# A sliding-window attention and MLP-mixer kernel: u turned by DMA in five of eight batches, and the hand-written order rewritten

## Chip, cores, metric

The kernel runs on one core of one Trainium2 chip. The metric is the device time of one execution in microseconds (us). Twelve executions of the kernel before gave a median of 300.88 us (298.99 to 302.43).

## What is computed

The reference, cut to what matters:

```
q, k, v: [8 batches, 8 heads, 576 tokens, 64]        float32
scores = q @ k.T / 8 + alibi bias, kept where 0 <= i - j < 128
attn   = softmax(scores);  x = (attn @ v) as [8, 576, 512]
h  = relu(x.T @ w_tok1) @ w_tok2        w_tok1 576x256, w_tok2 256x576
u  = x + h.T
h2 = relu(u @ w_ch1) @ w_ch2            w_ch1 512x1536, w_ch2 1536x512
out = u + h2
```

Only a band of 128 tokens takes part in each row of scores, so the two channel products (the last line but one) are most of the arithmetic.

## The kernel before

576 tokens are four chunks of 128 and a tail of 64. The work of each batch is cut into named steps, and five strings (PROLOGUE, FIRST, SECOND, PERIOD, LAST; lines 23 to 47) say by hand in which order the steps are issued. PERIOD is run for batches 2 to 6. A name without a tick is a step of the current batch b; each tick adds one batch, so `S20''` in batch b is a score step of batch b + 2. There is no scheduler: every engine runs its instructions in the order in which the strings issue them, and a step that waits holds up what stands behind it on the same engine. `emit` (line 809) walks the strings.

The steps, with the engine and the line of their main instruction:

- `q l` (193), `v` and `L` (183, 186), `LW`, `G`, `H` (665, 693, 732): loads from HBM with a cast to bf16, issued on POOL. `q`, `l` load a pair or two pairs of heads of q and k for batches 0 and 1; `Lq`, `Lk` load q and k of a later batch by tokens into `qn`, `kn` (four loads of 128 tokens and a tail each); `v0` to `v4` load v; `LW` loads w_tok1 and w_tok2; `G0` to `G2` load thirds of w_ch1 (512 KB each in SBUF), `H0`, `H1` halves of w_ch2 (768 KB each). The first two head pairs of batch 0 come in float32 on SP's queue (723) and are cast by DVE and ACT (`cq`, `ck`, 728).
- `M`, `m`: masks of the alibi bias, from `dist` that `J` makes on POOL. `I` makes the identity.
- `A`, `AT` (227, 252): TensorE turns q and k of batches 0 and 1 by head pair. `Zq`, `Zk` (211, 214): for batches 2 to 7 DMA transposes on SP's queue turn `qn`, `kn` into `qT`, `kT`.
- `S`kb j (280 to 293): scores of key chunk kb for four heads (j) on TensorE, exp on ACT out of a PSUM pair `psS`, product with the mask on DVE (299) one step later.
- `p` (572), `P` (339, 343, 371): attention times v. The first is by head pair, for batch 0, the others by query chunk. DVE takes reciprocals of the sums (587, 352) and scales.
- `k`, `K` (610, 404): first token product. `u`, `U`, `UT` (628, 429, 440): second token product, with x added on DVE (431), which gives `ub`, that is u.
- `x`, `X` (645, 461): u is turned, 128 x 128 blocks at a time, into `utb`, as `C` needs it with channels on the partitions. TensorE does it: four transposes for a chunk of 128 tokens, then one copy out of PSUM by ACT or DVE (464). A batch has four such chunks, X0 to X3.
- `C` (471) and `T` (486): channel product 1, twelve steps of four matmuls of 512 columns; the relu goes to DVE for the numbers in DVE_RELU (474), else to ACT (477).
- `D` (519) and `E` (541): channel product 2, three parts a chunk, four matmuls of 512 columns a part; DVE adds u (524) and SP's queue stores (525).
- `W`n (656): n matmuls on zeros that nobody reads.

PSUM has two pairs `psS` and three single tiles `psM` in rotation. SP's queue carries the float32 loads, the DMA transposes and the output stores, in the order of the strings. POOL carries all other loads. `utrans` (448) holds both ways of turning u: for batches in U_DMA it issues one DMA transpose for two chunks (451), at X0 and X2, and nothing at X1 and X3. In the kernel before, U_DMA is empty.

Of the kernel before, what the change touches and what calls it, by code (L numbers as in the profile page):

```python
# [10 lines left out]
ACT = mybir.ActivationFunctionType  # L11
# [4 lines left out]
PE_BATCHES = 2  # L16
CH2_PARTS = 3
MASK_LATER = 1
U_DMA = ()
U_ACT = (0,)  # L20
X_DVE = (3,)
K_DVE = (1,)
PROLOGUE = """
l1 O q0 I J q23 M0 l0 l23 FC qt G0 M1 m0 ck1 v0 cq0 M2 v1 LC q1 ck0 M3 cq1 v2 A0 v3 A1 S00 v4
S20 A2 AT S10 A3 m1 S30 LW q01' G1 q23' S21 S01 S11 W1 p0 l01' l23' p1 k0 v1' S31 k1 v3' qt' G2
v1'' u0 u1 Lk'' v4' v2' p2 x1 v0' p3 H1 H0 Lq'' k2 x0 u2 k3 v3'' ek A0' v4''' u3
"""
FIRST = """
UT x2 A2' v4'' x3 e1 A3' C4 C6 v0'' Zk'' Zq'' AT' S21' S11' A1' Lq''' T1 C1 C8 ex S00' S01' C9
C2 S20' C7 P0' T0 S10' C3 S30' S31' e2 C5 v2'' C0 v2''' Lk''' P1' C11 v0''' C10 P3' D00 P2' D01  # L30
P4' v3''' v1''' D02 E2 K0' K1' D10 D11 U1' D12 U3' X1' U2' UT' D20 D21 E1 U0' D30 S11'' S00''
D31 S10'' D22 S01'' T1' D32 E0 S20'' X3' X0' P0'' Zq'''
"""
SECOND = """
X2 T0 v4''' Zk'' P1' C5 S30' C3 C11 C0 Lk''' S31' S21' C9 C2 C7 C10 C6 P3' C1 v0''' C8 v2''' C4
v3''' D00 D01 P2' P4' D02 Lq''' K0' v1''' S01'' S20'' K1' D10 D11 D12 U3' U2' UT' U1' U0' X2'
S11'' S10'' X1' D20 X0' D21 D22 S21'' S00'' D30 E0 E1 X3' E2 D31 D32 P0''
# [7 lines left out]
C0 C6 C7 C1 C3 C2 C8 C5 C11 C4 C9 C10 D00 D20 D21 D10 T0 D01 D02 D22 D11 D12 T1 E0 E1 E2 D30 D31  # L45
D32
"""
VROW = 96
NPB = 9
SPLIT = (0, 2, 3, 5, 7)  # L50
x_DVE = (1, 2, 3)
k_DVE = (0, 1)
AK_DVE = (0, 3, 4, 5, 6, 7)
AQ_ACT = (0, 4, 6)
DVE_RELU = (2, 3, 6, 8, 10, 11)


@with_exitstack
def kernel(
# [102 lines left out]
    def later(n, fn):  # L162
        pend.append([n, fn])
# [94 lines left out]

    qrot = [0]
    probs = {}  # L260
    tok1_banks = {}

    def score(b, kb, j):

        i = b % 2

        def f():
            n = qrot[0]  # L270
# [286 lines left out]
    def pv_hp(hp):  # L557
        def f():
            E = 2 * (D + 1)
            vt = vp[0]  # L560
            psO = S2()
            for bank in range(2):
                first = True
                for qb in (2 * bank, 2 * bank + 1):
                    for i in range(2):
                        oi = psO[:, bank, (qb % 2) * E + i * (D + 1):(qb % 2) * E + (i + 1) * (D + 1)]
                        if qb > 0:
                            nc.tensor.matmul(
                                oi, lhsT=prob(0, qb - 1, 2 * hp + i, 1),
                                rhs=vt[:, qb - 1, 2 * hp + i, 0:D + 1], start=first, stop=False)  # L570
# [165 lines left out]
    def names(b):  # L736
# [40 lines left out]
        if b == 0:  # L777
# [74 lines left out]
```

The softmax here doesn't subtract the row's maximum and nothing guards it: scores larger than these inputs give would overflow.

## Time and profile before

| | |
|---|---|
| median of 12 executions | 300.88 us |
| the profiled execution | 299.84 us |
| its span on the core | 298.1 us |
| TensorE (PE) busy | 282.9 us, 95% |
| VectorE (DVE) busy | 172.7 us, 58% |
| ScalarE (ACT) busy | 129.0 us, 43% |
| POOL busy, with its load instructions | 99.6 us, 33% |
| mean granted TensorE clock | 0.989 |

The profile page is read as follows. A row of 40 digits cuts the span into equal slices (7.45 us here) and gives the busy share in tenths; PEclk is the granted TensorE clock in tenths of full speed. Group lines name the line, the engine, the operation, out<-in, the shape and the count, then busy time and mean duration, then idle time of the engine just before them and what ended it. The mean duration of a matmul is its latency; consecutive matmuls overlap, so what one costs a busy TensorE is the distance of starts. The chain of waits follows the run back from its last instruction; its pieces, given as start and length, don't overlap, so they show this distance.

### The profile page before, as it was taken

The page shows a single profiled execution, that of the slowest core. Times are in us where ns is not written, and L with a number is a line of the kernel's source. Part 1 is how long each engine was busy: PE and PEld are TensorE (multiplying, and loading weights), DVE is VectorE, ACT ScalarE, POOL GpSimd, SP SyncE. Part 2 cuts the span into 40 slices and gives each one's busy share as a digit, 9 for nine tenths or more (in the row PEclk, how much of TensorE's full clock was granted, in tenths as well). Part 3 has the DMA queues.
Part 4 walks back from the last instruction along what each step waited for, and adds up shares of the span by engine and source line. Part 5 has one row for each costly group of instructions (what it writes and reads, how often), then busy time and mean ns, then how long its engine had stood idle before and what let it go on. Part 6 is the DMA issues. An engine that isn't in the chain of part 4 may idle for free.

```text
span 298.1 us, 6583 instructions
## 1 busy us (share of the span) xinstructions
PE 282.9 (95%) x2757; PEld 159.5 (54%) x2757; DVE 172.7 (58%) x341; ACT 129.0 (43%) x203; POOL 99.6 (33%) x128
## 2 busy tenths in 40 slices
PE   1989997999999999999999999999999999999995
PEld 0568654546455456555564556555554556554453
DVE  2788776547756546485647636485647536543221
ACT  6853784038415534245615444345515444022210
POOL 8776871159209808800690008600000000000000
PEclk9969999999999999999999999999999999999999
DMA  7999999999999999952999169913501120110023
GB/s 175 178 194 185 172 180 159 147 167 180 129 145 141 174 206 157 142 94 77 177 155 134 42 150 158 142 52 114 118 2 70 49 61 0 36 72 35 2 90 86
DMA packets 138076, 35.38 MB, mean 119 GB/s; under 512 B 125248, under 2 KB 133568, under 8 KB 138048
## 3 DMA queue, kind: packets, MB, share of 16 engines
q0 software_dynamic: 103152, 17.41, 77.0%
q1 hardware_dynamic: 34896, 17.57, 25.3%
q8 instruction: 21, 0.34, 0.5%
q14 instruction: 7, 0.06, 0.1%
HBM read 35.85 MB, written 9.44 MB: 152 GB/s over the span
## 4 chain that ended last, share of the span: by engine, by line
PE 82%; DMA 12%; ACT 2%; POOL 1%; issue 1%; DVE 1%; SPq 0%
PE psM L519 27%; PE psM L471 25%; DMA WC<-in_moe_w_ch_dram 11%; PE psM L429 4%; PE psM L404 4%; PE psS L280 4%; PE psM L541 3%; PE psT L486 3%; PE psM L461 2%; PE psS L343 2%; DMA kf<-in_k_dram 2%; PE psS L339 2%; ACT pe L293 1%; PE psS L371 1%; PE psM L500 1%; PE psM L413 1%
## 5 line engine op out<-in xcount | busy, mean ns | idle before, releaser
L471 PE MATMUL psM<-utb,WC 128*128 128x512 bf16 x384 | 90.2, 379 | 0.2 <-ACT r L477 0.2
L519 PE MATMUL psM<-WC,r 128*128 128x512 bf16 x372 | 88.2, 379 | 1.8 <-DMA WC<-in_moe_w_ch_dram 1.8
L293 ACT ACTIVATE pe<-psS 128x1024 bf16<-128x1024 f32 (+1 forms) x69 | 62.7, 964 | 37.4 <-PE psS L280 30.0
L519 PEld LDWEIGHTS <-r 128*128 128x128 bf16 x372 | 34.3, 98 | 40.2 <-issue 4.4
L471 PEld LDWEIGHTS <-WC 128*128 128x128 bf16 x384 | 34.7, 98 | 37.5 <-issue 1.6
L474 DVE TENSOR_SCALAR r<-psM 128x512 bf16<-128x512 f32 x48 | 33.2, 691 | 27.5 <-PE psM L471 27.4
L299 DVE TENSOR_TENSOR pb<-pe,masks 128x1024 bf16<-128x1024 bf16 (+1 forms) x51 | 33.3, 658 | 21.0 <-ACT pe L293 20.9
L183 POOL DMA_DIRECT2D kn<-in_k_dram x24 | 21.1, 903 | 64.2 <-DMA kT<-kn 63.2
L477 ACT ACTIVATE r<-psM 128x512 bf16<-128x512 f32 x48 | 27.8, 601 | 27.3 <-PE psM L471 27.2
L524 DVE TENSOR_TENSOR ob<-psM,ub 128x512 f32<-128x512 f32 x31 | 21.4, 691 | 27.0 <-PE psM L519 26.7
L183 POOL DMA_DIRECT2D vp<-in_v_dram x32 | 29.0, 945 | 3.9 <-DMA qn<-in_q_dram 2.3
L183 POOL DMA_DIRECT2D qn<-in_q_dram x24 | 21.2, 918 | 9.6 <-DMA qT<-qn 9.6
L431 DVE TENSOR_TENSOR ub<-psM,xb 128x512 bf16<-128x512 f32 x28 | 18.7, 683 | 3.8 <-PE psM L429 3.8
L464 ACT COPY utb<-psM 128x512 bf16<-128x512 bf16 x21 | 12.3, 597 | 19.8 <-PE psM L461 19.7
L489 ACT ACTIVATE r2t<-psT 128x384 bf16<-128x384 f32 x16 | 7.9, 492 | 28.7 <-PE psT L486 28.7
L353 DVE TENSOR_TENSOR xb<-psS,rt 128x512 bf16<-128x512 f32 x28 | 19.4, 691 | 1.0
L280 PE MATMUL psS<-qT,kT 64*128 64x256 bf16 x192 | 16.5, 280 | 1.3 <-ACT pe L293 0.6
L422 ACT ACTIVATE r<-psM 128x512 bf16<-128x512 f32 x7 | 4.2, 598 | 27.5 <-PE psM L413 27.5
L343 PE MATMUL psS<-vp,pb 128*128 128x65 bf16 x224 | 15.7, 193 | 0.0
L429 PE MATMUL psM<-r,W 128*128 128x512 bf16 x56 | 15.4, 381 | 0.0
L343 PEld LDWEIGHTS <-pb 128*128 128x128 bf16 x224 | 13.6, 97 | 3.4
L352 DVE RECIPROCAL rt<-psS 128x8 f32<-128x8 f32 x28 | 5.7, 204 | 15.1 <-PE psS L343 15.1
(119 smaller groups left out, 321.1 us busy)
## 6 DMA issues: line engine op xcount, KB each, us to landing
out_dram<-ob SPq DMA_DIRECT2D x31, 256.0 KB, 2.0
vp<-in_v_dram POOLq DMA_DIRECT2D x32, 128.0 KB, 5.7
kn<-in_k_dram POOLq DMA_DIRECT2D x24, 128.0 KB, 5.3
qn<-in_q_dram POOLq DMA_DIRECT2D x24, 128.0 KB, 4.8
WC<-in_moe_w_ch_dram POOLq DMA_DIRECT2D x3, 512.0 KB, 8.4
WC<-in_moe_w_ch_dram POOLq DMA_DIRECT2D x2, 768.0 KB, 12.0
out_dram<-ob SPq DMA_DIRECT2D x10, 128.0 KB, 2.3
qs<-in_q_dram POOLq DMA_DIRECT2D x3, 256.0 KB, 6.6
```

The costliest lines, as they stand in the source:

```text
L183: nc.gpsimd.dma_start(out=dst, in_=src[b, :, c * P:(c + 1) * P, :].rearrange("h s d -> s h d"))
L280: nc.tensor.matmul(s[:, h, a * 256:(a + 1) * 256], lhsT=kT[i][r, kb, hp, :], rhs=qT[i][r, kb:kb + 2, hp, :], start=True, stop=True)
L293: nc.scalar.activation(out=e[:, h, :], in_=s[:, h, :], func=ACT.Exp, scale=scale)
L299: nc.vector.tensor_tensor(out=p[:, :].rearrange("p (h x) -> p h x", h=2)[:, h], in0=e[:, h, :], in1=masks[:, j, h].rearrange("p h g a x -> ...
L343: nc.tensor.matmul(ov, lhsT=prob(b, qb, h, 0), rhs=vt[:, qb, h, 0:D + 1], start=first, stop=(hh == 3))
L353: nc.vector.tensor_tensor(out=xb[b % 2][:, qb, :].rearrange("p (b h d) -> p b h d", b=2, h=4), in0=ov[:, :, :, 0:D], in1=rv[:, :, :, None] ...
L429: nc.tensor.matmul(t[:, :], lhsT=W2[:, j, c * P:(c + 1) * P], rhs=r1[b % 2][:, j, :], start=(j == 0), stop=(j == 1))
L471: nc.tensor.matmul(t[:, :], lhsT=WC1[:, cb, ht * P:(ht + 1) * P], rhs=utb[b % 2][:, :, cb, :], start=(cb == 0), stop=(cb == NCB - 1))
L474: nc.vector.tensor_scalar(out=r2[b % 2][:, ht, :], in0=t[:, :], scalar1=0.0, scalar2=None, op0=ALU.max)
L477: nc.scalar.activation(out=r2[b % 2][:, ht, :], in_=t[:, :], func=ACT.Relu)
L519: nc.tensor.matmul(t[:, :], lhsT=r2[b % 2][:, ht, c * P:(c + 1) * P], rhs=WC2[:, ht, :], start=(ht == 0), stop=(ht == NHT - 1))
L524: nc.vector.tensor_tensor(out=o[:, :], in0=t[:, :], in1=ub[b % 2][:, c, :], op=ALU.add)
```

## The change

Settings and orders are changed, one step is added, and two functions are edited:

- U_DMA becomes (3, 4, 5, 6, 7): in these batches u is turned by two DMA transposes (X2 first, then X0) on SP's queue. Batches 0, 1 and 2 keep TensorE.
- In PERIOD `Zq''` and `Zk''` stand together, `Zq''` first, ahead of the loads `Lk'''` and `Lq'''`; FIRST has the order `Lk'' Lq''`, then `Zq'' Zk''`, then `Lk''' ...`. X stands earlier in PERIOD.
- In PROLOGUE and FIRST all loads of w_ch1 and w_ch2 and of batch 1 stand ahead of the q, k and v of batch 2; the tokens' weights (`LW`) stand ahead of the first w_ch1 third. Fifteen matmuls on zeros (`W`) are issued instead of one, nine of them before `A0`. `A0'` to `A3'`, `AT'`, `S00'`, `S01'`, `S10'` and `T0` stand before the first `C`, which is now `C8`.
- The first score step of batch 0 is cut in two, by head pair (`s0`, `t0`); four score steps of batch 0 use two `psM` tiles instead of a `psS` pair, and all are exponentiated by halves.
- `pv_hp` takes one reciprocal of 12 columns instead of two of 4 and 6.
- Sharing between DVE and ACT is redone; DVE_RELU has eight numbers instead of six.

```diff
-U_DMA = ()
+U_DMA = (3, 4, 5, 6, 7)
...
-X_DVE = (3,)
-K_DVE = (1,)
+X_DVE = (1, 3)
+K_DVE = (0,)
 PROLOGUE = """
-l1 O q0 I J q23 M0 l0 l23 FC qt G0 M1 m0 ck1 v0 cq0 M2 v1 LC q1 ck0 M3 cq1 v2 A0 v3 A1 S00 v4
-S20 A2 AT S10 A3 m1 S30 LW q01' G1 q23' S21 S01 S11 W1 p0 l01' l23' p1 k0 v1' S31 k1 v3' qt' G2
-v1'' u0 u1 Lk'' v4' v2' p2 x1 v0' p3 H1 H0 Lq'' k2 x0 u2 k3 v3'' ek A0' v4''' u3
+J M3 FC l23 M0 M1 W1 q0 q23 I l0 M2 cq0 W1 ck0 m0 l1 O q1 ck1 cq1 qt W3 v0 W4 A0 W3 v1 v2 s0 A1
+W2 S20 v3 t0 A2 AT v4 S10 LW A3 S30 m1 S01 l01' S11 q01' p0 G1 l23' p1 G0 W1 qt' e1 S31 k0 q23'
+S21 G2 H0 k1 v2' ek LC p2 A1' H1 A0' p3 u0 k2 u1 x0 v3' v4' k3 u2
 """
 FIRST = """
-UT x2 A2' v4'' x3 e1 A3' C4 C6 v0'' Zk'' Zq'' AT' S21' S11' A1' Lq''' T1 C1 C8 ex S00' S01' C9
...
+x1 v0' ex u3 A3' A2' AT' v1' Lk'' Lq'' UT x2 S00' S01' x3 Zq'' Zk'' T0 Lk''' S10' C8 v0'' v3''
+C9 Lq''' S20' v0''' S21' v4'' C3 e2 C5 S31' S11' C0 C2 S30' C4 v2'' v4''' C7 P0' C11 P2' T1 C1
+C10 C6 E0 D00 P1' D01 P3' D02 v1'' v2''' P4' K0' K1' D10 E2 U1' D11 D12 Zq''' U2' v1''' UT' X1'
+U0' D30 D20 S20'' S11'' D21 D31 D32 Zk''' E1 D22 S01'' U3' S00'' X2'
 """
...
 PERIOD = """
-P1' T0 Zk'' C1 C6 C9 C10 S30' S31' C0 Zq'' C4 C7 P3' C5 P2' C3 C8 v1''' T1 C11 v3''' Lk''' P4'
-C2 K0' Lq''' K1' v2''' D00 D01 D02 v4''' S01'' S00'' U0' U2' D10 v0''' D11 D12 U1' S21'' S11''
-U3' D20 X1' D21 P0'' D22 X0' UT' S20'' S10'' X2' X3' D30 D31 D32 E0 E1 E2
+C7 T0 C4 C3 C0 S31' S30' Zq'' C8 C2 Zk'' C11 C9 P1' C1 C10 P2' P3' Lk''' C6 C5 Lq''' P4' v0'''
+K0' K1' S01'' S00'' D00 v2''' v1''' D01 D02 T1 U2' U1' UT' U0' v3''' U3' D20 X2' X3' X1' D21
+P0'' D10 D11 v4''' S11'' S10'' X0' D12 D30 D22 D31 S20'' S21'' E0 E1 D32 E2
 """
...
-SPLIT = (0, 2, 3, 5, 7)
+SPLIT = (1, 2, 3, 4)
+S_M = (0, 5, 6, 7)
...
-DVE_RELU = (2, 3, 6, 8, 10, 11)
+DVE_RELU = (0, 2, 3, 4, 5, 7, 10, 11)
...
+    def score_half(kb, a):
+        def f():
+            if a == 0:
+                n = qrot[0]
+                qrot[0] += 1
+                half[kb] = (S2(), pe[n % len(pe)], pb[n % len(pb)])
+                probs[0, kb, 0] = half[kb][2]
+            s, e, p = half[kb]
+            cs = slice(a * 256, (a + 1) * 256)
+            for h in range(2):
+                r = slice(h * D, (h + 1) * D)
+                nc.tensor.matmul(s[:, h, cs], lhsT=kT[0][r, kb, a, :],
+                                 rhs=qT[0][r, kb:kb + 2, a, :], start=True, stop=True)
+            nc.scalar.activation(out=e[:, :, cs], in_=s[:, :, cs], func=ACT.Exp, scale=scale)
...
-            s = S2()
+            apart = b == 0 and j * 4 + kb in S_M
+            t2 = None if apart else S2()
+            s = [M(), M()] if apart else [t2[:, 0, :], t2[:, 1, :]]
...
-                for bank, n in ((0, 4), (1, 6)):
-                    nc.vector.reciprocal(
-                        out=r[:, bank * 4:bank * 4 + n, None],
-                        in_=psO[:, bank, 0:n * (D + 1)].rearrange("p (h e) -> p h e", h=n)[:, :, D:D + 1])
+                rv = r[:, :].rearrange("p (b h) -> p b h", b=2)
+                nc.vector.reciprocal(
+                    out=rv[:, :, :, None],
+                    in_=psO[:, :, 0:6 * (D + 1)].rearrange("p b (h e) -> p b h e", h=6)[:, :, :, D:D + 1])
```

More of the change, by code (lines that the diff above doesn't have):

```diff
@@ L27 @@
+W2 S20 v3 t0 A2 AT v4 S10 LW A3 S30 m1 S01 l01' S11 q01' p0 G1 l23' p1 G0 W1 qt' e1 S31 k0 q23'
+S21 G2 H0 k1 v2' ek LC p2 A1' H1 A0' p3 u0 k2 u1 x0 v3' v4' k3 u2
 """
 FIRST = """
-UT x2 A2' v4'' x3 e1 A3' C4 C6 v0'' Zk'' Zq'' AT' S21' S11' A1' Lq''' T1 C1 C8 ex S00' S01' C9
-C2 S20' C7 P0' T0 S10' C3 S30' S31' e2 C5 v2'' C0 v2''' Lk''' P1' C11 v0''' C10 P3' D00 P2' D01
-P4' v3''' v1''' D02 E2 K0' K1' D10 D11 U1' D12 U3' X1' U2' UT' D20 D21 E1 U0' D30 S11'' S00''
-D31 S10'' D22 S01'' T1' D32 E0 S20'' X3' X0' P0'' Zq'''
+x1 v0' ex u3 A3' A2' AT' v1' Lk'' Lq'' UT x2 S00' S01' x3 Zq'' Zk'' T0 Lk''' S10' C8 v0'' v3''
@@ L33 @@
+C9 Lq''' S20' v0''' S21' v4'' C3 e2 C5 S31' S11' C0 C2 S30' C4 v2'' v4''' C7 P0' C11 P2' T1 C1
+C10 C6 E0 D00 P1' D01 P3' D02 v1'' v2''' P4' K0' K1' D10 E2 U1' D11 D12 Zq''' U2' v1''' UT' X1'
+U0' D30 D20 S20'' S11'' D21 D31 D32 Zk''' E1 D22 S01'' U3' S00'' X2'
 """
 SECOND = """
-X2 T0 v4''' Zk'' P1' C5 S30' C3 C11 C0 Lk''' S31' S21' C9 C2 C7 C10 C6 P3' C1 v0''' C8 v2''' C4
-v3''' D00 D01 P2' P4' D02 Lq''' K0' v1''' S01'' S20'' K1' D10 D11 D12 U3' U2' UT' U1' U0' X2'
-S11'' S10'' X1' D20 X0' D21 D22 S21'' S00'' D30 E0 E1 X3' E2 D31 D32 P0''
+X3 X0 T1 S30' S10' C3 C1 T0 C2 P0' C8 Lk''' C7 v3'' C5 S31' S21' C11 Lq''' v2''' C4 C10 C0 P4'
@@ L38 @@
+v0''' v4''' C9 C6 D00 P1' v3''' P3' D01 P2' D02 v1''' K0' K1' S01'' S20'' D10 D11 D12 U2' UT'
+U0' U3' S00'' U1' X0' S11'' X2' D20 D21 E0 S21'' S10'' D22 E1 X1' E2 P0'' D30 X3' D31 D32
 """
 PERIOD = """
-P1' T0 Zk'' C1 C6 C9 C10 S30' S31' C0 Zq'' C4 C7 P3' C5 P2' C3 C8 v1''' T1 C11 v3''' Lk''' P4'
-C2 K0' Lq''' K1' v2''' D00 D01 D02 v4''' S01'' S00'' U0' U2' D10 v0''' D11 D12 U1' S21'' S11''
-U3' D20 X1' D21 P0'' D22 X0' UT' S20'' S10'' X2' X3' D30 D31 D32 E0 E1 E2
+C7 T0 C4 C3 C0 S31' S30' Zq'' C8 C2 Zk'' C11 C9 P1' C1 C10 P2' P3' Lk''' C6 C5 Lq''' P4' v0'''
@@ L43 @@
+K0' K1' S01'' S00'' D00 v2''' v1''' D01 D02 T1 U2' U1' UT' U0' v3''' U3' D20 X2' X3' X1' D21
+P0'' D10 D11 v4''' S11'' S10'' X0' D12 D30 D22 D31 S20'' S21'' E0 E1 D32 E2
 """
 LAST = """
-C0 C6 C7 C1 C3 C2 C8 C5 C11 C4 C9 C10 D00 D20 D21 D10 T0 D01 D02 D22 D11 D12 T1 E0 E1 E2 D30 D31
+C7 T1 C0 C1 C2 C9 C6 C8 C10 C11 C4 C3 T0 C5 D00 E0 D01 D10 D02 E1 D11 D20 D21 D22 E2 D12 D30 D31
 D32
@@ L49 @@
 NPB = 9
-SPLIT = (0, 2, 3, 5, 7)
+SPLIT = (1, 2, 3, 4)
+S_M = (0, 5, 6, 7)
 x_DVE = (1, 2, 3)
-k_DVE = (0, 1)
-AK_DVE = (0, 3, 4, 5, 6, 7)
-AQ_ACT = (0, 4, 6)
-DVE_RELU = (2, 3, 6, 8, 10, 11)
+k_DVE = (0, 1, 3)
+AK_DVE = (2,)
+AQ_ACT = (0, 1, 4, 5, 7)
+DVE_RELU = (0, 2, 3, 4, 5, 7, 10, 11)
 @with_exitstack
@@ L260, with g @@
     probs = {}
+    half = {}
+    def score_half(kb, a):
[12 more added lines that the diff above has]
+            nc.scalar.activation(out=e[:, :, cs], in_=s[:, :, cs], func=ACT.Exp, scale=scale)
+            def g():
+                nc.vector.tensor_tensor(
+                    out=p[:, :].rearrange("p (h x) -> p h x", h=2)[:, :, cs], in0=e[:, :, cs],
+                    in1=masks[:, 0, :, a].rearrange("p h g x -> p h (g x)"), op=ALU.mult)
+            later(MASK_LATER, g)
+        return f
     tok1_banks = {}
@@ L279, in f @@
                     for h, r in enumerate(halves):
-                        nc.tensor.matmul(s[:, h, a * 256:(a + 1) * 256], lhsT=kT[i][r, kb, hp, :],
+                        nc.tensor.matmul(s[h][:, a * 256:(a + 1) * 256], lhsT=kT[i][r, kb, hp, :],
                                          rhs=qT[i][r, kb:kb + 2, hp, :], start=True, stop=True)
@@ L283, in f @@
                 for h, r in enumerate(halves):
-                    nc.tensor.matmul(s[:, h, a * P:(a + 1) * P], lhsT=kT[i][r, kb, hp, :],
+                    nc.tensor.matmul(s[h][:, a * P:(a + 1) * P], lhsT=kT[i][r, kb, hp, :],
                                      rhs=qT[i][r, kb, hp, :], start=True, stop=True)
@@ L288, in f @@
                         c = 256 + t * P + a * ST
-                        nc.tensor.matmul(s[:, h, c:c + ST], lhsT=kT[i][r, kb + t, hp, :],
+                        nc.tensor.matmul(s[h][:, c:c + ST], lhsT=kT[i][r, kb + t, hp, :],
                                          rhs=qT[i][r, NC, hp, 0:ST], start=True, stop=True)
-            parts = (slice(0, 1), slice(1, 2)) if b == 0 and j * 4 + kb in SPLIT else (slice(0, 2),)
-            for h in parts:
-                nc.scalar.activation(out=e[:, h, :], in_=s[:, h, :], func=ACT.Exp, scale=scale)
+            split = apart or b == 0 and j * 4 + kb in SPLIT
+            parts = (slice(0, 1), slice(1, 2)) if split else (slice(0, 2),)
+            for n, h in enumerate(parts):
+                nc.scalar.activation(out=e[:, h, :], in_=s[n][:, None, :] if split else t2[:, :, :],
+                                     func=ACT.Exp, scale=scale)
             probs[b, kb, j] = p
@@ L592, in g @@
                     in0=psO[:, :, 0:2 * E].rearrange("p b (q i e) -> p b q i e", q=2, i=2)[:, :, :, :, 0:D],
-                    in1=r[:, 0:8].rearrange("p (b q i) -> p b q i", b=2, q=2)[:, :, :, :, None].broadcast_to([P, 2, 2, 2, D]),
+                    in1=rv[:, :, 0:4].rearrange("p b (q i) -> p b q i", q=2)[:, :, :, :, None].broadcast_to([P, 2, 2, 2, D]),
                     op=ALU.mult)
-                nc.vector.tensor_tensor(out=rtt[:, :], in0=r[:, 8:10], in1=hm[:, :], op=ALU.mult)
+                nc.vector.tensor_tensor(out=rtt[:, :], in0=r[:, 10:12], in1=hm[:, :], op=ALU.mult)
                 nc.vector.tensor_tensor(
@@ L796, in names @@
             d["O"] = lambda: ones_v(0)
+            for kb in range(NC - 1):
+                d[f"s{kb}"], d[f"t{kb}"] = score_half(kb, 0), score_half(kb, 1)
             for j in range(2):
```

## The prediction

> **What bounds the kernel now.** First the page: which engine is full, and where not.
>
> ```profile
> PE 282.9 (95%) x2757; PEld 159.5 (54%) x2757; DVE 172.7 (58%) x341; ACT 129.0 (43%) x203; POOL 99.6 (33%) x128
> ...
> PE   1989997999999999999999999999999999999995
> ...
> PEclk9969999999999999999999999999999999999999
> DMA  7999999999999999952999169913501120110023
> ```
>
> TensorE is full except in the first seven slices (52 us) and in the last. The clock dips in the third slice. The DMA engines are full for 17 slices and mostly free from slice 31. Next the busy time by stretch (columns: PE, PEld, DVE, ACT, POOL, clock, DMA share, GB/s), cut at the first product (16.86), the first C (31.95), the first D (51.07) and, further on, at starts of periods:
>
> ```profile
> 16.86:31.95 15.09, 13.97 (x229) 11.97 (x228) 12.25 (x36) 6.40 (x14) 11.00 (x15) 0.78 1.53 193
> 31.95:51.07 19.12, 17.11 (x207) 9.28 (x205) 14.35 (x27) 13.85 (x21) 10.28 (x13) 1.00 1.70 168
> 106.15:138.20 32.05, 32.05 (x318) 17.82 (x315) 20.65 (x39) 14.38 (x21) 12.57 (x15) 1.00 1.29 139
> 138.20:173.06 34.86, 34.86 (x334) 19.22 (x331) 20.33 (x38) 14.81 (x22) 12.56 (x15) 1.00 1.08 124
> ```
>
> A period holds 32.05 us of work on TensorE and no idle time; an odd batch has E as well and takes 34.86 us. So in PERIOD only what leaves TensorE counts. Then the chain of waits, in order of time (start, length):
>
> ```profile
> 25.00 8.83 DMA WC<-in_moe_w_ch_dram
> ...
> 36.67 14.36 DMA WC<-in_moe_w_ch_dram
> 51.07 1.02 PE psM L519 x4
> ...
> 166.62 0.55 PE psM L461 x8
> 167.17 2.59 PE psM L519 x12
> ```
>
> Up to 51 us the loads set the pace: the last third of w_ch1 lands at 33.83, the last half of w_ch2 at 51.03, and D starts with it (TensorE waits 1.81 us there, by the list of waits). After that all is TensorE. A transposing matmul of u costs 0.55/8 = 0.069 us in the chain, a matmul of 512 columns 2.59/12 = 0.216, though the groups give their latency:
>
> ```profile
> L461 PE MATMUL psM<-ident,ub 128*128 128x128 bf16 x112 | 9.9, 220 | 0.6 <-DVE ob L524 0.6
> L464 ACT COPY utb<-psM 128x512 bf16<-128x512 bf16 x21 | 12.3, 597 | 19.8 <-PE psM L461 19.7
> ```
>
> Last, the DMA transposes of q and k, issued on SP's queue (start, length of the issue), and their landings:
>
> ```profile
> 38.15 8.01 SPq L211 DMA_TRANSPOSE kT<-kn  x1
> ...
> 71.06 5.06 SPq L211 DMA_TRANSPOSE qT<-qn  x1
> ...
> 174.58 1.45 SPq L211 DMA_TRANSPOSE kT<-kn  x1
> ```
> ```profile
> DMA to landing us min/median/max: 3.6/5.2/15.7
> ```
>
> One of these turns 16 blocks of 128 x 128. The 3.6 to 6.3 us are those from 106 us on; the 15.7 and 12.4 us are those issued at 38.15 and 71.06, with loads in full flight.
>
> **What the Trainium skill says.** "TensorE: Matmul & The Clock Gate", What's actually happening: the array runs at half clock until about 3.4 us of sustained work, and falls back after an idle window. The trace agrees: eight 128-column transposes took 0.64 us at 4.92 and 0.41 us at 28.29, and the third slice was granted 0.6. "VectorE: DVE Perf Modes", The three transpose paths: 1309 ns for a 128 x 128 block by DMA, 390 ns by TensorE. The trace disagrees for batches of blocks: 16 in 3.6 us by DMA, and 69 ns each for a busy TensorE; I use the trace. "DMA: Bandwidth & Descriptors", Issuing engines are not separate DMA queues: transfers of SP and POOL share the 16 DMA engines. The spread from 3.6 to 15.7 us agrees.
>
> **The change, part by part.** (1) *u of five batches leaves TensorE.* 5 x 16 transposes x 0.069 = 5.5 us, all from full stretches: -5.5. The wait of 0.37 us of TensorE just before the last X (start of 266.68 in the chain) goes too: -0.4. Twenty copies out of PSUM (0.42 to 0.60 us) leave ACT and DVE, which weren't the bound: nothing.
>
> (2) *Ten DMA transposes come, and C waits for both of a batch.* The listing of instructions shows them on SP between the store of D0 and that of D1; X0 waits for nothing of its own, so it is issued as soon as X2's issue ends, not at its place in the string. Each is half of one for q or k. The pair is therefore taken as one of 16 blocks: 3.6 to 6.3 us. Time that covers it: X2 waits for DVE's add of u (U3'), done about 0.4 us into D21. From there to C7 TensorE has eight D parts less 0.4 (8 x 0.86 - 0.4), four scores (0.27 each) and P0'' (0.25): 7.8 us, and 2.9 more in odd batches (E). So nothing: 0, with 1.5 us to spare. Behind them on SP stand only stores of D1 to D3, for which `ob` has four buffers. The loads of a period landed by 22.8 us after its start (106.15 to 128.98); now k's and q's transposes both precede them, some 4 us later; X2 is issued at about 23. So the pair meets the last loads in batches 3 to 5. Bounds: 0 and, at 12.4 us, 4.6 us a batch in these three.
>
> (3) *Order of the loads.* Before the last third of w_ch1, two v loads of batch 1 leave (0.84 us apart in the landings): 33.83 - 1.7 = 32.2. The first C needs it now (C8), and so starts at 32.2, 0.25 later than before. But ahead of it TensorE has done in addition A1' (0.48), AT' (0.23), three scores (0.8) and T0 (0.70, the x24 of line 486) = 2.2 us. Net -1.9. It can be there in time: p0 came at 16.86, and can come at about 14.5, since the first transposes of k waited for ACT until 7.32 behind a load that now is second, and exp starts with half a step; from p0 to C8 are 12 us of work for 17.7 us. Warm-up matmuls: 9 x 0.43 cold = 3.9 us from 1.1 to 5.0, where TensorE had nothing before 4.92; six more lie in waits. Nothing; 0.5 if they outlast these. The one reciprocal saves 4 x 0.15 us of DVE in the same stretch: within the net, as loads set its end. Bounds for the start: 0 and -2.6 (0.7 for loads that land sooner).
>
> (4) *w_ch2 ahead of batch 2.* It lands at about 32.2 + 10.5 + 0.8 = 43.5; the D part that reads its end starts after 45. The 1.8 us go. What is late next: q and k of batch 2. By the landings before (0.84 a load) they arrive at 53.5; four transposes follow (issues 1.3, 1.2, 1.5, 1.2, the third landing 3.7 to 5 after its issue): 60. TensorE comes to S20'' after 24.4 us of work from C8, and loses some 2.8 us as before in short waits: 59.4. New wait 0.6 (0 to 3).
>
> (5) *Eight relus on DVE instead of six.* In PERIOD 2 x 0.69 us on an engine busy 20 of 35: nothing. In the C steps of batch 0, with eight scores to mask (0.66 each) between them, DVE has nearly as much as TensorE: +0.5 (0 to 2).
>
> Sum: -5.5 - 0.4 - 1.9 - 1.8 + 0.6 + 0.5 = -8.5. The profiled execution took 299.84 (span 298.1), so its like would take 291.3. The median shown is 1.04 above it: 300.88 - 8.5 = 292.4.
>
> **Rivals.** *Only u counts:* the new start waits elsewhere (DVE and ACT in the masks and copies, a half clock again) and gives back (3) and (4): 300.88 - 5.9 = 295.0. For it: ACT is busy 13.0 of the first 16.9 us. Against it: the load's time of 32.2 leaves 5 us of slack. *A little late:* each pair of u comes 1 us after C7 wants it: 292.4 + 5 = 297.4. For it: issues of up to 2.9 us in quiet times. Against it: the 1.5 us to spare. *Transposes among loads, slower than before:* in batches 3 to 5 the pair takes 12.4 us as the one at 71.06 did, stalls 4.6 us each, 13.8 in all: 292.4 + 13.8 = 306.2. It decides once the five pairs together stall more than 8.5 us. For it: the overlap with the last v loads in (2). Against it: only four or so of 15 loads are then left, and the transposes at 111.07 and 177.60, with loads issued just behind, took 5.4 and 6.3. *It cancels:* stalls of about that sum: 300.9. That the change doesn't do what it says is excluded by the listing: 80 transposes fewer, ten DMAs more.
>
> **How the numbers follow.** The forecast has 0.57, only u counts 0.19, a little late 0.12, it cancels 0.04, among loads 0.08. Low end: without (4)'s and (5)'s additions (-1.1), loads sooner (-0.7), and half of the other short waits between 32 and 65 us gone (-1.6): 289.0. High end: a little late, 297.4, which leaves the last two cases out. A measurement of this kernel tells about 0.3% (0.9 us) from no change. Faster 0.88, the same 0.04, slower 0.08.
>
> **What would show it.** Line 461's count falls from 112 to 32; periods last 30.9 and 33.8 us; no wait of TensorE on `utb` by DMA; the pair lands within 7.8 us. D starts without a wait for w_ch2; the first C is at 32 to 33 us; a wait of TensorE for kT before S20'' is under 3 us. A wait for `utb` in each period, or a first C after 34 us, would make the prediction wrong.

## The result and the profile after

The kernel after takes 291.86 us (median of 11 executions, 291.0 to 293.26), the kernel before beside it 300.62. The ratio is 0.9716 (95% interval 0.9697 to 0.9736), a gain of 8.5 us. Ratios here leave disturbed executions out and medians don't, and each is taken against the kernel before as run beside it (its median lay between 300.62 and 301.72), so that the two can differ, once by more than 1 us. Gains in us are worked out from the ratios, with 300.62 for the kernel before. The profiled execution took 291.69 us, its span is 290.0. First the page of the kernel after, the same rows as before:

```profile
PE 279.1 (96%) x2691; PEld 154.4 (53%) x2691; DVE 178.6 (62%) x349; ACT 114.4 (39%) x177; POOL 99.7 (34%) x128
...
PE   7778999999999999999999999999999999999995
...
PEclk9599999999999999999999999999999999999999
DMA  7999999999999997995999967995803320041014
```

TensorE is now full from the fifth slice (29 us) on; before it was from the eighth. The DMA row stays mostly full to slice 29 (210 us), before to slice 26. Next the busy time by stretch of the kernel after: from the first C (34.70) to the first D (48.58), and two periods.

```profile
34.70:48.58 13.88, 13.86 (x134) 6.88 (x133) 11.69 (x23) 9.44 (x14) 7.50 (x9) 1.00 2.07 170
103.50:134.45 30.95, 30.95 (x298) 16.96 (x296) 19.77 (x37) 11.03 (x16) 12.57 (x15) 1.00 1.37 155
134.45:168.20 33.75, 33.75 (x313) 18.34 (x312) 22.90 (x41) 12.73 (x17) 12.58 (x15) 1.00 1.25 139
```

A period takes 1.10 us less than before (32.05 and 34.86), which is 16 x 0.069. The stretch between the first C and the first D took 19.12 and takes 13.88. The transposes of u that TensorE still does, from the groups of the kernel after, and the landings of the DMA ones from the view of their line:

```profile
L490 PE MATMUL psM<-ident,ub 128*128 128x128 bf16 x32 | 3.0, 220 | 0.1
```
```profile
DMA to landing us min/median/max: 3.2/4.8/7.3
```

32 instead of 112. By the trace, the five pairs land 6.1, 8.6, 6.2, 4.45 and 4.46 us after X2's issue; the C step that reads them starts 8.4, 11.2, 8.4, 11.2 and 6.9 us after it. So every pair has 2.2 us or more to spare in this execution. Last, the longest waits of TensorE in the kernel after (total, times, longest):

```profile
PE psS L276 <- DVE qT L233: 2.7, 1, 2.7
PE psM L640 <- DVE rtt L625: 1.2, 1, 1.2
PE psT L686 <- DVE zt L681: 1.1, 1, 1.1
```

All three lie before the first C. Neither w_ch2, nor `utb`, nor kT of batch 2 is in the list.

**Where the 8.15 us of the two profiled executions lie.** The first D comes 2.5 us earlier (51.07 to 48.58). Before it the order of after has some 0.7 us less of work, so 1.8 are gained there. From the first D to the end it takes 241.4 us instead of 247.0, with that 0.7 in addition: 6.3 gained. But the first C is late: 34.70, not 32 to 33. Two pieces of the timeline of the kernel after tell why (start, length, engine, line; in brackets the wait before it). On DVE:

```profile
8.21 0.68 DVE L758 CAST qs<-qf 128x512 bf16<-128x512 f32 x1 [2.66 <-DMA qf<-in_q_dram]
8.81 0.74 DVE L233 COPY qT<-psM 128x256 bf16<-128x256 bf16 x2
```

and on TensorE:

```profile
9.27 0.40 PE L276 MATMUL psS<-qT,kT 64*128 64x256 bf16 x2 [2.73 <-DVE qT L233]
...
30.34 0.41 PE L228 MATMUL psM<-ident,qs 128*64 128x128 bf16 x8
...
34.70 1.91 PE L500 MATMUL psM<-utb,WC 128*128 128x512 bf16 x8
```

The first score step waits for a copy on DVE that stands behind the cast of the second float32 load of q, which landed at 8.19 (7.41 before). And `A3'` starts at 30.34, just after the second load of q of batch 1 (`q23'`) landed at 30.19. Its weight load shows the wait:

```profile
30.23 0.36 PEld L228 LDWEIGHTS <-qs 128*64 128x64 bf16 x8 [0.18 <-DMA qs<-in_q_dram]
```

The wait is short here: TensorE, with p0 at 17.24, came to `A3'` when the load was about to land. Between `A3'` and C8 stand 4.4 us of work. The last third of w_ch1, which the prediction took for the bound, landed at 32.46 and held up nothing.

### The profile page after: what moved, and what is told of

It is laid out like the page before. It is cut to its first block, busy times and chain, and to the rows that moved or that the text cites. A ratio compares the mean times of both kernels' runs of the same rounds, so it can differ in the third digit from the quotient of the medians.

```text
span 290.0 us, 6418 instructions
## 1 busy us (share of the span) xinstructions
PE 279.1 (96%) x2691; PEld 154.4 (53%) x2691; DVE 178.6 (62%) x349; ACT 114.4 (39%) x177; POOL 99.7 (34%) x128
## 4 chain that ended last, share of the span: by engine, by line
PE 90%; DVE 4%; DMA 2%; ACT 1%; issue 1%; SPq 0%; ACTq 0%; DVEq 0%
PE psM L500 29%; PE psM L548 28%; PE psM L458 4%; PE psM L433 4%; PE psS L307 4%; PE psT L515 4%; PE psM L570 4%; PE psS L372 2%; DMA qf<-in_q_dram 2%; PE psS L368 2%; PE psS L400 1%; ACT pe L321 1%; PE psM L529 1%; PE psS L311 1%; PE psM L228 1%; PE psM L442 1%
## 5 line engine op out<-in xcount | busy, mean ns | idle before, releaser
L548 PE MATMUL psM<-WC,r 128*128 128x512 bf16 x372 | 87.1, 379 | 0.0
L321 ACT ACTIVATE pe<-psS 128x1024 bf16<-128x1024 f32 (+1 forms) x64 | 58.9, 973 | 49.1 <-PE psS L307 35.3
L500 PEld LDWEIGHTS <-WC 128*128 128x128 bf16 x384 | 35.1, 98 | 38.6 <-issue 1.1
L503 DVE TENSOR_SCALAR r<-psM 128x512 bf16<-128x512 f32 x64 | 43.3, 688 | 19.8 <-PE psM L500 19.8
L506 ACT ACTIVATE r<-psM 128x512 bf16<-128x512 f32 x32 | 19.1, 602 | 30.3 <-PE psM L500 30.3
L518 ACT ACTIVATE r2t<-psT 128x384 bf16<-128x384 f32 x16 | 7.9, 494 | 32.3 <-PE psT L515 32.2
L460 DVE TENSOR_TENSOR ub<-psM,xb 128x512 bf16<-128x512 f32 x28 | 17.8, 687 | 3.1 <-PE psM L458 3.1
L307 PE MATMUL psS<-qT,kT 64*128 64x256 bf16 x180 | 15.2, 277 | 0.8 <-DVE qT L233 0.8
L372 PE MATMUL psS<-vp,pb 128*128 128x65 bf16 x224 | 15.1, 193 | 0.0
L458 PE MATMUL psM<-r,W 128*128 128x512 bf16 x56 | 14.9, 380 | 0.0
L515 PEld LDWEIGHTS <-WC 128*128 128x128 bf16 x384 | 13.2, 98 | 3.1
L451 ACT ACTIVATE r<-psM 128x512 bf16<-128x512 f32 x7 | 4.2, 598 | 25.2 <-PE psM L442 25.2
L515 PE MATMUL psT<-utt,WC 128*128 128x64 bf16 x384 | 13.8, 193 | 0.0
```

Source lines behind the costliest of these rows:

```text
L307: nc.tensor.matmul(s[h][:, a * 256:(a + 1) * 256], lhsT=kT[i][r, kb, hp, :], rhs=qT[i][r, kb:kb + 2, hp, :], start=True, stop=True)
L321: nc.scalar.activation(out=e[:, h, :], in_=s[n][:, None, :] if split else t2[:, :, :], func=ACT.Exp, scale=scale)
L372: nc.tensor.matmul(ov, lhsT=prob(b, qb, h, 0), rhs=vt[:, qb, h, 0:D + 1], start=first, stop=(hh == 3))
L458: nc.tensor.matmul(t[:, :], lhsT=W2[:, j, c * P:(c + 1) * P], rhs=r1[b % 2][:, j, :], start=(j == 0), stop=(j == 1))
L500: nc.tensor.matmul(t[:, :], lhsT=WC1[:, cb, ht * P:(ht + 1) * P], rhs=utb[b % 2][:, :, cb, :], start=(cb == 0), stop=(cb == NCB - 1))
L503: nc.vector.tensor_scalar(out=r2[b % 2][:, ht, :], in0=t[:, :], scalar1=0.0, scalar2=None, op0=ALU.max)
```

## The experiments

The theory before them: PERIOD with u by DMA gives 5.9 us, the start the rest, and the two add up. Rivals: one half gives all; the reordered loads alone, or the DMA alone, would do it; the pairs of u have room enough, or are just in time. Each kernel is given by its edit. "On after" means after's settings and lines.

**The start alone.** After's start with before's PERIOD and LAST, and no u by DMA:

```diff
-U_DMA = (3, 4, 5, 6, 7)
+U_DMA = ()
...
-C7 T0 C4 C3 C0 S31' S30' Zq'' C8 C2 Zk'' C11 C9 P1' C1 C10 P2' P3' Lk''' C6 C5 Lq''' P4' v0'''
...
+P1' T0 Zk'' C1 C6 C9 C10 S30' S31' C0 Zq'' C4 C7 P3' C5 P2' C3 C8 v1''' T1 C11 v3''' Lk''' P4'
...
```

> The order of the start (PROLOGUE, FIRST, SECOND) and all settings of the changed kernel, but PERIOD and LAST of the kernel before and no DMA for u. Theory (the two halves are independent, u is worth 80 x 0.069 + 0.4 = 5.9 us): the start is worth the rest of 8.8, that is 2.9: about 297.7. Rival (the order of PERIOD is itself worth something, the start little): 299.5 to 300.5. Rival (the start is worth the 3.7 of the prediction's terms for the first C and for w_ch2, and the DMA of u less than 5.9): 296.9 or less.

297.66 us, ratio 0.9909 (0.9876 to 0.9943): -2.7 us. The start gives about a third of the gain. What is missing to after, 0.0193 or 5.8 us, is u and PERIOD. "Only u counts" falls. This kernel has all the small edits in it (reciprocal, halves of the scores, other sharing); none of them was run by itself.

**PERIOD alone.** Before's start and settings, DVE_RELU with its six numbers among them, with after's PERIOD, LAST and U_DMA:

```diff
-U_DMA = ()
+U_DMA = (3, 4, 5, 6, 7)
...
-P1' T0 Zk'' C1 C6 C9 C10 S30' S31' C0 Zq'' C4 C7 P3' C5 P2' C3 C8 v1''' T1 C11 v3''' Lk''' P4'
...
+C7 T0 C4 C3 C0 S31' S30' Zq'' C8 C2 Zk'' C11 C9 P1' C1 C10 P2' P3' Lk''' C6 C5 Lq''' P4' v0'''
...
```

> The kernel before with PERIOD, LAST and U_DMA of the changed kernel; its own start and settings, so six relus on DVE. Theory: 300.6 - 5.9 = 294.7, no wait of TensorE on utb. Rival (DMA of u is paid for by late pairs or by stores and transposes of q and k held up on SP): 297 or more. If start and period are independent, the savings of this run and of start_only add up to 8.8.

298.59 us, 0.9942 (0.9919 to 0.9964): only -1.7 us. A miss. The pairs of u are not at fault, as no wait for them is in the list. What is there, from the waits of TensorE of this kernel:

```profile
PE psM L471 <- DVE r L474: 2.6, 4, 0.7
```

Once in each of four periods C waits 0.65 us for a relu on DVE. The new order of the C steps goes with the new sharing of the relus.

**The same with eight relus on DVE:**

```diff
-DVE_RELU = (2, 3, 6, 8, 10, 11)
+DVE_RELU = (0, 2, 3, 4, 5, 7, 10, 11)
```

> period_only with the eight relus on DVE of the changed kernel added, the start still that of before. Theory (the sharing is what period_only lacked): 300.7 - 5.9 = 294.8, no wait of TensorE for a relu in PERIOD. Rival (the old start does not go with the new period): about 298.6 as period_only.

296.19 us, 0.9824 (0.9783 to 0.9866): -5.3 us, with -5.9 inside the interval. The wait for the relu is gone. With the start's -2.7 this makes -8.0, against -8.5 for the whole: within the intervals the halves add up. (The eight relus stand in both.) The new order without the DMA of u was not run. By the profiles TensorE has no idle time in a period before or after, so that the 1.10 us are the work taken away; but how much the order would give alone is open.

**After with six relus:**

```diff
-DVE_RELU = (0, 2, 3, 4, 5, 7, 10, 11)
+DVE_RELU = (2, 3, 6, 8, 10, 11)
```

> The changed kernel with the six relus on DVE of the kernel before (DVE_RELU = 2, 3, 6, 8, 10, 11). The prediction charged eight relus with +0.5: then 291.4. Theory after period_only (the new order of C needs the new sharing; there TensorE waited in four periods for a relu): some 3.7 slower than the changed kernel, 295.6, with waits of TensorE for line 503 in PERIOD. Rival (period_only lost its 3.7 by something else, such as the start): 291.4 to 292.4.

295.68 us, 0.9799 (0.9765 to 0.9834): 2.5 us above after, by the ratios. The same four waits of 0.65 us are back, 2.6 in all. So the sharing is worth about 2.5 us where the prediction had a cost.

**u by DMA in the old order.** Before with one line changed:

```diff
-U_DMA = ()
+U_DMA = (3, 4, 5, 6, 7)
```

> The kernel before with one setting changed: U_DMA = (3, 4, 5, 6, 7), all orders as before. There X0 and X2 stand behind the store of D2 on SP and X2 is followed by only some 3.8 us of TensorE's work before C1 in even batches and 6.6 in odd ones. The pair needed 4.5 to 8.6 us in the changed kernel. Theory (the cover of 7.8 us is what makes the DMA free): waits of TensorE on utb of 1 to 2.5 us in each even batch and 0 to 2 in odd ones, some 5 in all, so about 300. Rival (the place does not matter, a pair is there soon): 294.7.

303.99 us, 1.0099 (1.0064 to 1.0134): 3.0 us slower than before, with 80 transposes less on TensorE. From its waits:

```profile
PE psM L471 <- DMA utb<-ub: 5.3, 3, 3.0
```

The pairs took 4.5 to 5.7 us there, no longer than in after. What lacks is cover: X2 stands near the end of the old PERIOD. After the longest wait the trace shows TensorE at half clock from 274.2 to 277.6. This profiled execution (304.77) lies 4.9 us above that of before. Some 2.4 of them lie before the first C of batch 1, where nothing was edited: the wait for w_ch2 was 2.6 instead of 1.8, and half clock followed from 52.3 to 55.8. The other 2.6, near the 3.0 of the ratio, come later: odd periods gain 0.9 each, even ones lose 0.5, and the end, from batch 6 on, with its half clock loses 3.4. So it is not the DMA by itself that gains, but the DMA with X moved ahead.

**X moved back in after.** X2 and X0 behind D12, which on SP's queue means behind the store of D1:

```diff
-K0' K1' S01'' S00'' D00 v2''' v1''' D01 D02 T1 U2' U1' UT' U0' v3''' U3' D20 X2' X3' X1' D21
-P0'' D10 D11 v4''' S11'' S10'' X0' D12 D30 D22 D31 S20'' S21'' E0 E1 D32 E2
+K0' K1' S01'' S00'' D00 v2''' v1''' D01 D02 T1 U2' U1' UT' U0' v3''' U3' D20 X3' X1' D21
+P0'' D10 D11 v4''' S11'' S10'' D12 X2' X0' D30 D22 D31 S20'' S21'' E0 E1 D32 E2
```

> The changed kernel with the DMA transposes of u behind the store of D1 on SP instead of ahead of it: X2 is then issued some 4.6 us later, when D1's sum is done. Theory (what is free is free because of the cover): of 8.4, 11.2, 8.4, 11.2 and 6.9 us from X2's issue to C7 in the changed kernel, 4.6 go; pairs take 4.5 us when no load is in flight; waits of about 0.7, 0, 0.7, 0 and 2.2 us: 295.5. It loses more where TensorE's clock falls after such a wait. Rival (the pair has more room than that, or stores cost more than transposes): 291.9.

303.02 us (299.45 to 304.93), 1.0032 (1.0006 to 1.0057): 1.0 us slower than before by the ratio, and 9.5 us above after. That it is slower than after was expected, the size was not. From the timeline of TensorE:

```profile
136.68 1.85 PE L500 MATMUL psM<-utb,WC 128*128 128x512 bf16 x4 [2.33 <-DMA utb<-ub]
...
205.54 1.02 PE L500 MATMUL psM<-utb,WC 128*128 128x512 bf16 x4 [2.37 <-DMA utb<-ub]
...
270.90 1.02 PE L500 MATMUL psM<-utb,WC 128*128 128x512 bf16 x4 [2.48 <-DMA utb<-ub]
```

X2 of batch 3 was issued at 131.97 instead of 126.06, so that only 2.4 of the 8.4 us of cover are left, and the pair took 4.6 us. That is faster than in after (6.1): the last load had landed 1.8 us before X2. So the wait comes from the place of the issue and not from the transfer. The other part is the clock: four matmuls that take 1.02 us elsewhere took 1.85 after the first wait. The stretch of busy time around it (columns as before, the clock third from the right):

```profile
135.00:140.00 5.00, 3.32 (x29) 2.01 (x30) 1.91 (x4) 0.36 (x2) 0.00 (x0) 0.67 1.04 262
```

A window of 3.4 us (136.7 to 140.1) at half clock costs 1.7 us of work. Three waits (7.2) and one such window (1.7) are 8.9 of the 9.2 us by which this profiled execution (300.91) lies above after's (291.69). Other executions of this kernel fit: with a mean clock of 0.989 over the run they took 299.5 to 301.1 us, with 0.983 301.0 to 301.9, with 0.977 302.2 to 303.9. Each 0.0057 of 300 us is 1.7 us, that is one more such window. The mean clock doesn't order the executions of every kernel so: of the kernel before, those with 0.994 took 299.7 to 303.0.

**u by DMA one batch earlier,** on after:

```diff
-U_DMA = (3, 4, 5, 6, 7)
+U_DMA = (2, 3, 4, 5, 6, 7)
```

> The changed kernel with u of batch 2 turned by DMA as well (U_DMA from 2 on). Theory (16 transposes less in a full stretch, some 8.4 us of cover from X0' to C7 in SECOND): -1.1, 290.8. Rival (loads are still in full flight at 95 us, and the pair takes 9 to 12 us there): a wait of 1 to 4 us, and the clock with it, 292 to 296.

295.58 us, 0.9831 (0.9789 to 0.9873): 3.5 us above after, though 1.1 us more leaves TensorE. Its timeline shows two waits of C:

```profile
105.66 1.02 PE L500 MATMUL psM<-utb,WC 128*128 128x512 bf16 x4 [2.25 <-DMA utb<-ub]
...
139.40 1.02 PE L500 MATMUL psM<-utb,WC 128*128 128x512 bf16 x4 [2.64 <-DMA utb<-ub]
```

The pair of batch 2, issued at 94.85 among loads of q and v, took 10.7 us. The second wait is a consequence: the issue of the q transpose ahead on SP's queue took 5.2 us instead of 1.9, the k transpose of the next period landed 4.2 us later than in after (117.28 for 113.07), and the loads of k that wait for it left 4.2 us later (117.81 for 113.60). X2 of batch 3 came only 2.3 us later (128.37 for 126.06). So the pair, which takes 6.1 us in after, had more of these loads beside it and took 10.9. This is the prediction's slow rival, transposes among loads, one batch further up. "DMA: Bandwidth & Descriptors" of the Trainium skill (Issuing engines are not separate DMA queues) says that transfers of all issuing engines interleave on the same 16 DMA engines; the two durations of the same transfer, 6.1 and 10.9, agree.

**w_ch2 early, in before.** H1 and H0 right behind the last third of w_ch1:

```diff
-S20 A2 AT S10 A3 m1 S30 LW q01' G1 q23' S21 S01 S11 W1 p0 l01' l23' p1 k0 v1' S31 k1 v3' qt' G2
-v1'' u0 u1 Lk'' v4' v2' p2 x1 v0' p3 H1 H0 Lq'' k2 x0 u2 k3 v3'' ek A0' v4''' u3
+S20 A2 AT S10 A3 m1 S30 LW q01' G1 q23' S21 S01 S11 W1 p0 l01' l23' p1 k0 v1' S31 k1 v3' qt' G2 H1 H0
+v1'' u0 u1 Lk'' v4' v2' p2 x1 v0' p3 Lq'' k2 x0 u2 k3 v3'' ek A0' v4''' u3
```

> The kernel before with the two loads of w_ch2 moved ahead of v1'' and Lk'' in PROLOGUE, nothing else. Theory: TensorE's wait of 1.8 us before the first D goes and nothing takes its place, since the loads of batch 2 end when they did: 298.8, between 298.3 and 299.2. Rival (the wait turns into one for kT and qT of batch 2): 300.6.

306.89 us, 1.0214 (1.0178 to 1.0249): 6.4 us slower, by neither theory. The wait for w_ch2 is gone; in its place the waits have

```profile
PE psS L343 <- DMA vp<-in_v_dram: 8.0, 1, 8.0
```

The halves had been set ahead of v of batch 1, and the attention of batch 1, which comes before the first D, now waits for that.

**Only the k of batch 2 behind w_ch2, in before:**

```diff
-v1'' u0 u1 Lk'' v4' v2' p2 x1 v0' p3 H1 H0 Lq'' k2 x0 u2 k3 v3'' ek A0' v4''' u3
+v1'' u0 u1 v4' v2' p2 x1 v0' p3 H1 H0 Lk'' Lq'' k2 x0 u2 k3 v3'' ek A0' v4''' u3
```

> The kernel before with the five loads Lk'' (k of batch 2) moved behind the loads of w_ch2 in PROLOGUE, so that w_ch2 is 3.8 us earlier and the v loads of batch 1 stay where they were. Theory (the w_ch2 wait alone, with nothing in its place): -1.8, so 298.9 against 300.7. Rival (what wch2_first showed: a load that is passed is the next to be waited for, here k of batch 2, whose transposes now end later): 300.7 or more.

298.78 us, 0.9924 (0.9902 to 0.9945): -2.3 us. D starts at 48.63 instead of 51.07 without a wait, and the list has a small new one:

```profile
PE psS L280 <- DMA kT<-kn: 1.2, 1, 1.2
```

This is step (4) of the prediction by itself, with the new wait that it named (0.6 there, 1.2 here). In the two profiled executions 2.4 us are gained before D and 1.2 of them lost again in this wait (298.64 against 299.84); the ratio over all executions gives more, and that was not taken apart. Passing k of batch 2, which isn't needed until 60 us, is what gains; passing v of batch 1 is what loses.

**The casts behind the first transposes, on after** (`ck1 cq1` behind `A0`, so that the copy of qT doesn't stand behind the cast on DVE):

```diff
-J M3 FC l23 M0 M1 W1 q0 q23 I l0 M2 cq0 W1 ck0 m0 l1 O q1 ck1 cq1 qt W3 v0 W4 A0 W3 v1 v2 s0 A1
+J M3 FC l23 M0 M1 W1 q0 q23 I l0 M2 cq0 W1 ck0 m0 l1 O q1 qt W3 v0 W4 A0 ck1 cq1 W3 v1 v2 s0 A1
```

> The changed kernel with ck1 and cq1 moved behind A0: the copies of the first transposes no longer stand behind casts that wait for the second float32 loads. Theory (the first C at 34.7 instead of 32.2 is due to waits of DVE and ACT at the start, this one of 2.7 us among them): TensorE comes to s0 some 2 us sooner; later scores wait for the second head pair all the same, so 0.5 to 1.2 of it reaches the end: 290.7 to 291.4. Rival (the loads or the exps behind set the first C): 291.9. Rival (the second pair's copies now come later): 292.4.

291.99 us, 0.9688 (0.9651 to 0.9724): the interval overlaps that of after. The wait of 2.7 us for the score is gone, and

```profile
PE psM L228 <- DVE qs L758: 2.4, 1, 2.4
```

has come: the next step, A1, needs the same cast. The first C is at 34.96.

**The second pair taken for landed, on after.** The casts read the tile of the first pair, so q and k of heads 2 and 3 of batch 0 are replaced by those of heads 0 and 1; all loads are still issued:

```diff
-        cp(out=dst[:, hs, :], in_=src[:, hs, :])
+        cp(out=dst[:, hs, :], in_=src[:, 0:2, :])
```

> The changed kernel, but the casts of the second float32 pair of heads (cq1, ck1) read the tile of the first pair; its loads are still issued and land unread. This replaces q and k of heads 2 and 3 of batch 0 by those of heads 0 and 1, so that part of the computation is another; work and loads are the same. It takes away the wait for the second float32 load (8.19 us) that held up s0 and, in casts_later, A1. Theory (that load sets the late p0 of 17.2 us): p0 at about 15, the first C at 33 or sooner, the total 289.5 to 290.6. Rival (the exps of ACT and the copies of DVE behind it set p0 anyway): p0 at 16.5 or later, 291.5 to 292.2.

292.07 us, 0.9686 (0.9649 to 0.9722): nothing gained. The first score starts at 6.46 instead of 9.27, and p0 at 15.72 instead of 17.24. Then, on its timeline:

```profile
10.90 0.64 PE L228 MATMUL psM<-ident,qs 128*64 128x128 bf16 x8 [2.46 <-DMA qs<-in_q_dram]
...
30.68 0.41 PE L228 MATMUL psM<-ident,qs 128*64 128x128 bf16 x8 [1.32 <-DMA qs<-in_q_dram]
```

A2 waits for the load `q23` of batch 0, and A3' for `q23'` of batch 1. The first C comes at 35.04, 4.4 us after `q23'` landed (30.63). The same distance holds in all eight kernels with after's start: the first C lay between 34.17 and 35.58 and the landing of `q23'` between 29.75 and 31.10, and the difference of the two was always 4.4 to 4.6 us. `A3'` started within 0.25 us of the landing in all eight, though p0 lay anywhere from 15.72 to 18.12. No kernel moved `q23'` alone, so what an earlier one would bring was not shown.

**No matmuls on zeros, on after** (the 15 `W` matmuls taken out of PROLOGUE):

```diff
-J M3 FC l23 M0 M1 W1 q0 q23 I l0 M2 cq0 W1 ck0 m0 l1 O q1 ck1 cq1 qt W3 v0 W4 A0 W3 v1 v2 s0 A1
-W2 S20 v3 t0 A2 AT v4 S10 LW A3 S30 m1 S01 l01' S11 q01' p0 G1 l23' p1 G0 W1 qt' e1 S31 k0 q23'
+J M3 FC l23 M0 M1 q0 q23 I l0 M2 cq0 ck0 m0 l1 O q1 ck1 cq1 qt v0 A0 v1 v2 s0 A1
+S20 v3 t0 A2 AT v4 S10 LW A3 S30 m1 S01 l01' S11 q01' p0 G1 l23' p1 G0 qt' e1 S31 k0 q23'
```

> The changed kernel without its fifteen matmuls on zeros. Theory (they lie in waits, and the clock falls to half after them anyway, from 8 to 15 us in the profile): 291.9 to 292.6. Rival (the clock that they hold up is part of the gain): 293.5 or more. Rival (they cost time on TensorE): 291.0 or less.

292.34 us, 0.9733 (0.9699 to 0.9767): not to be told from after. The clock record is full only from 14.6 us on here, and in after from 4.7 to 8.1 and again from 14.9. The first C is at 34.32, as `q23'` landed at 29.75. And the pair of batch 3 was late here, though PERIOD is that of after: it took 9.0 us, and the weights of C7 show the wait.

```profile
134.77 0.56 PEld L500 LDWEIGHTS <-WC 128*128 128x128 bf16 x4 [1.20 <-DMA utb<-ub]
```

TensorE stood idle for 0.7 us there. (The list of waits puts this down to a product with the mask on DVE; in after the same product ended later than C7 started, so it isn't the cause.) So the 2.2 us to spare in after's profile don't hold in every execution. Still, none of the kernels tried is faster than after beyond what its interval tells.

## Why the prediction was right, and where it wasn't

Against its sum of -8.5 stand -8.5 by the ratio (7.9 to 9.1) and -8.15 in the two profiled executions. The agreement is better than the steps are, and in part luck.

- **(1) u off TensorE: right.** 1.10 us in each period, as priced at 0.069 us a transpose; with the short waits that went, 5.9 from the start of the first PERIOD to the start of LAST (164.2 us before, 158.35 after), for 5.9. This needs the relu sharing of (5).
- **(2) The DMA pairs cost nothing: right, in after's profile.** The cover was 6.9 to 11.2 us for the forecast 7.8 (10.7 in odd batches). The pairs took 4.45 to 8.6 us, and the 8.6 lay in an odd period, where E added to the cover. 2.2 us to spare where 1.5 had been worked out. Without the matmuls on zeros, with the same PERIOD, a pair was late all the same and cost 0.7. That the margin is small was shown by three kernels: X moved back, the old order, and u from batch 2 on; each turned much of the gain, or all of it, into waits.
- **(3) First C at 32.2, -1.9 net: wrong.** The landing of the last third of w_ch1 was right (32.46 for 32.2), but another load was the bound: "It can be there in time: p0 came at 16.86, and can come at about 14.5". p0 came at 17.24, and C8 had to wait for `A3'`, whose load landed at 30.2, and for 4.4 us of work behind it. The work was sized too small as well: 12 us from p0 to C8 were forecast, and TensorE is counted busy for 14.6 of these 17.5. With 2.2 us more done ahead and a first C 2.75 later, the step cost 0.5 instead of gaining 1.9. In the six kernels with before's steps ahead of the first C it lay at 30.7 to 32.3, in the eight with after's at 34.2 or later, so this isn't one execution's chance. The prediction checked the load that C8 itself reads, not those of the steps that the change had put ahead of C8. By its own words, a first C after 34 us makes it wrong; for this step it does.
- **(4) w_ch2 without a wait: right,** -1.8, and -2.3 when done by itself. Its addition of 0.6 for kT of batch 2 didn't come in after: TensorE waited for nothing there, with kT landed at 59.2; q of batch 2 had landed at 51.55, not 53.5. Where k alone was moved, it came, with 1.2.
- **(5) Eight relus +0.5: wrong in sign.** By an estimate that prices the work with the distances of starts in the profile of before, TensorE lost some 3.4 us in the C stage before, 1.8 of it for w_ch2 and so 1.6 in short waits; after it loses some 0.9 (13.9 us for 13.0 of work). That is -0.7 in this stage. The relus explain little of it: with six of them after's C stage took 14.07 us (34.42 to 48.49) for 13.88. The rest would be the order. In the periods, "an engine busy 20 of 35: nothing" was the fallacy of the mean: with six relus the new order waits 0.65 us a period.

The two misses, +2.4 in (3) and -1.2 in the C stage at (5), with -0.6 in (4), nearly cancel: that is the luck. What is left, some -0.4 from the first D on, lies in short waits and was not taken apart. Of the rivals, "only u counts" needed the start to give nothing, and it gives 2.7; "transposes among loads" has a true mechanism that decides one batch earlier. What stays open, beside the small edits that were not run alone, is why the float32 load of q landed 0.8 us later than before: POOL's loads were issued 0.4 us sooner (2.16 for 2.58), but no kernel changed that alone.

## What to carry to other kernels

Moving work from a full engine to a DMA pays when the issue is moved ahead by the transfer's time: the DMA gave +3.0 us in the old order, and -5.3 together with the new order and its sharing of the relus. When steps are put ahead of a stage, check the loads of each of these steps and the work between their landing and the stage, not only the load that the stage itself reads. A transfer late in its period also decides when the next loads leave, so that one late pair makes the next one late.

## What the runs showed of the hardware

- A wait of TensorE of 2.33 us was followed by 3.4 us at half clock, one of 3.0 us too, and one of 2.6 us (for w_ch2, in u by DMA in the old order); waits of 2.37, 2.48, 2.25 and 2.64 us in the same kind of place were not. What sets them apart is how a wait lies in the clock's windows. In all fourteen traces the stretches of the granted clock, but for the last that the end cuts short, are 3.41 us long or a multiple of it: a grid of windows, in each of which TensorE's idle time can be counted. Four windows of X moved back in after, from its first and second wait (columns as before):

```profile
133.32:136.73 3.41, 1.08 (x7) 0.38 (x6) 1.89 (x3) 1.89 (x2) 0.00 (x0) 1.00 1.05 247
136.73:140.15 3.42, 3.42 (x30) 2.05 (x31) 0.69 (x1) 0.30 (x1) 0.00 (x0) 0.50 0.97 231
...
201.59:205.00 3.41, 1.58 (x12) 0.61 (x12) 1.86 (x3) 1.94 (x2) 0.00 (x0) 1.00 1.04 224
205.00:208.41 3.41, 2.87 (x35) 1.71 (x36) 0.96 (x3) 0.49 (x1) 0.00 (x0) 1.00 1.10 288
```

  The wait of 2.33 us lay in one window, the longer one of 2.37 was shared by two. From 30 us on, in all fourteen, every full-clock window with at most 1.92 us of idle TensorE was followed by full clock, and each of the four with 2.06 to 2.70 by half clock. In the first 30 us, where the matmuls are short, the clock fell after windows with as little as 1.2 us idle, so this limit was seen in the later stages alone. "TensorE: Matmul & The Clock Gate" of the Trainium skill (What's actually happening) has a free-running window of about 3.4 us, and half clock after an idle window. The length and the grid agree; that a window idle for some 60% is enough is more than the page says. Such a wait can cost up to 1.7 us more than its length.
- 16 blocks of 128 x 128 by DMA took 4.4 to 4.6 us with no loads about (most often; once 5.7), 6.1 to 8.6 at the end of the loads in after, and 10.7 to 10.9 among them in u from batch 2 on; SP's queue was held 1.2 to 4.0 us for each half. How far the loads are ahead goes with it: in the kernels with after's PERIOD a pair took 4.5 us where the first of the period's loads had left 14.4 us before X2, 6.1 at 12.5, 9.0 at 11.5 and 10.9 at 10.6.
- In this kernel a passed load came back as the next wait: in three kernels the wait that an edit had taken away (1.8 us for w_ch2, 2.7 us before the first score in two kernels) was followed by one of 8.0, 2.4 and 3.8 us on the load or cast that was next.
